# A new instruction order for a linear-attention and feed-forward kernel: w2 issued third by third behind w1, other chunks transposed by DMA

## The chip, the cores and the metric

The kernel runs on one core of a Trainium2 chip. The metric is the device time of one execution in microseconds (us). The inputs and the output are float32 in HBM; the matrix work on the core is done in bfloat16.

## What is computed

Two stages, one after the other, cut to what matters:

```
# stage 1: B=4, H=8 heads, S=768 steps, D=48; state is D x D per head
for t in range(S):
    y[:, :, t] = r_t @ (state + outer(u * k_t, v_t))
    state      = w * state + outer(k_t, v_t)
# stage 2: x = y as rows of C = 384
xn  = (x - mean) / sqrt(var + 1e-6) * g_ln
out = x + relu(xn @ w1) @ w2          # w1: 384 x 1536, w2: 1536 x 384
```

## The kernel before, in words

The 4 x 768 rows are cut into 24 chunks of 128 rows, six for each batch entry. Chunk i goes through a row of named steps, each a small function; the order of all steps is written out by hand in the string PLAN (lines 20 to 92), one entry "step,index,engine". Every engine runs its entries in this order and never overtakes (v is VectorE, DVE; s is ScalarE, ACT; g is GpSimd, POOL; a dash leaves the engine to the step: TensorE, PE, or the DMA queue of SyncE, SP). A loop at lines 651 to 653 only reads the string and calls the steps. An entry waits for whatever its data need; everything behind it on its engine waits too.

The steps of a chunk, in the order of its data:

- LK, LR, LV (lines 346 to 353) load k, r, v in 192-byte rows, 192 KB each, through SP's queue into rings of ten buffers.
- SK, SR (355 to 359) multiply k and r by powers of w into bf16 sck and scr. CV (361) casts v to vv.
- TR (364) transposes scr and sck on PE, eight matmuls against an identity; TC, TCr, TCk (371 to 378) copy the result from PSUM into trs. For chunks named in K_BY_DMA, TR does only scr and TKD (526) transposes sck by DMA; where the plan has TRD (530), scr goes by DMA too.
- Q (395) is an elementwise product for the u term in chunks 0 to 8. From chunk 9 on, KU and KR (389, 392) and a sum in CC replace it.
- AT (398) makes the 128 x 128 scores per head on PE, AM (426) masks them out of PSUM on DVE into A.
- S (429) makes the chunk's addition to the state in PSUM. ZU, ZD (460, 467) decay it into Z. For chunks in ZPE, PE adds the earlier Z itself by an identity matmul (line 441), so that ZU alone does it.
- VB (470), Y (476) and X (495) give x, with its row sum.
- SQ, XN, RS (501 to 520) do the normalization; g_ln is folded into w1.
- LT (534) and XT (539) transpose xn on PE and copy it out; LTD (522) does it by DMA instead.
- UP (543) multiplies by w1, RL (560) applies relu, DN (572) multiplies by w2, OT (634) adds, STO (641) stores. The last chunk is stored in two halves (DA, DB, OA, OB, SA, SB).

GROUPS joins chunks for UP: a group of one chunk does an UP of 12 matmuls of 128 columns, three of them covering the hidden width; a group of two does six UP of six matmuls of 256 columns. An entry UP,16g+m is part m of group g; DN,4i+d is third d of chunk i. UP's PSUM tile hp has two buffers, each freed by an RL.

The weights come in thirds. LW1 (line 329) loads a third of w1 (768 KB, 2 KB rows) on SP's queue. SW (332) scales one third of a third, index 3n+kc, into bf16 w1_sb on the engine that the plan names. IW2 (343) loads a third of w2 with a cast to bf16; it is issued from POOL and goes through POOL's own DMA queue. UP for a third of the hidden width needs that third's three SW; DN,4i+d needs third d of w2.

WU and DU are matmuls on zeros that nobody reads, put where PE would be idle.

Of the kernel before, what the change touches and what calls it, by code (L numbers as in the profile page):

```python
# [20 lines left out]
MW,0,v WF,0,- TL,0,s MI,0,g WU,13,- MP,0,v LN,0,s MM,0,g LK,0,- WBM,0,- RI,0,s LR,0,-
FR,0,s LV,1,- DU,4,- CL,0,- FK,0,s SR,0,v LK,2,- SK,0,v WL,0,s DU,3,- TR,0,- LR,1,-
UR,0,g TCk,0,v LK,1,- SK,2,g DU,2,- CU,0,- TCr,0,s SR,1,v LV,0,- Q,0,v AT,0,- UGC,0,s
LR,2,- SK,1,v AMb,0,v DU,3,- TR,1,- CV,0,s LK,3,- UW,0,s AMa,0,v S,0,- SR,2,v LV,2,-
Y,0,- TC,1,v CC,0,s LW1,1,- DU,9,- AT,1,- ZU,0,v VB,0,g Q,1,v CV,1,g X,0,v DU,9,-
TR,2,- CV,2,g S,1,- XN,0,g TC,2,s AM,1,v LR,3,- IW2,0,g SW,3,s LW1,0,- CC,1,v IW2,1,g
Q,2,v DU,13,- Y,1,- SW,4,s ZU,1,v LT,0,- VB,1,g SK,3,v SQ,0,s DU,1,- S,2,- SR,3,g
DU,1,- AT,2,- X,1,v XT,0,s AM,2,v XN,1,s SW,5,g DU,6,- TR,3,- CC,2,s SQ,1,s IW2,2,g
TC,3,v DU,1,- UP,1,- SW,2,v SW,1,s SW,0,g AT,3,- ZU,2,v LT,1,- RL,1,s Y,2,- AM,3,v
LV,3,- VB,2,g UP,0,- XT,1,s RS,0,g LK,4,- RL,0,s X,2,v DU,1,- UP,16,- CV,3,s XN,2,g  # L30
DN,0,- LW1,2,- RS,1,g SQ,2,s Q,3,v Y,3,- LT,2,- RL,16,s S,3,- SK,4,v XT,2,s CC,3,v
UP,33,- ZU,3,v VB,3,g UP,32,- RL,33,s SW,7,g X,3,v UP,17,- SW,8,g RL,32,v XN,3,s LR,4,-
RL,17,s SW,6,g LT,3,- LK,5,- DN,1,- XT,3,v RS,2,g UP,34,- SR,4,v LR,5,- SQ,3,s UP,2,-
RL,34,s RS,3,g SK,5,v LV,4,- TR,4,- RL,2,s UP,50,- SR,5,g TC,4,s UP,49,- RL,50,s AT,4,-
RL,49,s TR,5,- Q,4,v CV,4,s UP,18,- AM,4,v LV,5,- TC,5,s ZD,3,g S,4,- UP,48,- CC,4,v
LV,6,- VB,4,g ZU,4,v DN,2,- RL,48,s Q,5,v LR,6,- ZD,4,g Y,4,- OT,0,v AT,5,- RL,18,s
X,4,v S,5,- LK,6,- DN,4,- CV,5,g CC,5,v AM,5,v XN,4,s DN,5,- LK,7,- SQ,4,s VB,5,g
LT,4,- DN,6,- SR,6,v XT,4,s SK,6,g LR,7,- Y,5,- CV,6,v UP,65,- LUB,0,- UP,66,- SK,7,g
OT,1,v LR,8,- X,5,v TR,6,- RL,65,s DN,8,- SR,7,v LK,8,- TC,6,s RS,4,g RL,66,v UP,64,-
LV,7,- XN,5,v AT,6,- Q,6,v RL,64,s TR,7,- SR,8,v LR,9,- SK,8,g S,6,- TC,7,s DN,9,-  # L40
AM,6,v LK,9,- DN,10,- SQ,5,s CC,6,v Q,7,v LT,5,- LV,8,- VB,6,g CV,7,s Y,6,- ZU,6,v
AT,7,- XT,5,s OT,2,v S,7,- RS,5,g STO,1,- TR,8,- X,6,v LWB,0,- DN,12,- CC,7,v SK,9,v
XN,6,s VB,7,g LK,11,- DN,13,- ZU,7,v AM,7,v UP,82,- ZD,7,g LK,10,- TC,8,s DN,14,- UWR,0,v
SQ,6,s LK,12,- Y,7,- Q,8,v LT,6,- RL,82,s KU,9,v SR,9,g AT,8,- X,7,v STO,0,- XT,6,s
UP,80,- AM,8,v XN,7,s LV,10,- CV,8,g TR,9,- SQ,7,s SK,10,g S,8,- LK,13,- OT,3,v UP,81,-
TC,9,s KR,9,v RS,6,g Y,8,- SK,11,v LV,9,- DN,16,- RL,81,s KU,10,g LT,7,- LR,16,- DN,17,-
CC,8,v RL,80,v XT,7,s CV,9,s CC,9,v DN,18,- CV,10,g STO,2,- KU,11,v VB,8,g UP,101,- LR,10,-
ZU,8,v OT,4,v AT,9,- VB,9,g RL,101,s STO,3,- UP,98,- X,8,v LK,15,- AM,9,v S,9,- ZD,8,g
XN,8,s UP,96,- RL,98,s LV,11,- DN,20,- SK,12,v RL,96,s ZU,9,v Y,9,- SQ,8,s LK,18,- LT,8,-
SR,10,v UP,97,- ZD,9,g XT,8,s X,9,v LV,12,- DN,21,- KR,10,v RL,97,s S,10,- XN,9,v CV,11,s  # L50
TR,10,- LR,11,- KU,12,v DN,22,- CC,10,v SK,13,g TC,10,s LR,13,- ZU,10,v UP,100,- ZD,10,g UP,99,-
SQ,9,s LR,12,- OT,5,v LT,9,- RL,100,s AT,10,- VB,10,g LR,20,- XT,9,s DN,24,- AM,10,v SR,13,g
RL,99,s UP,112,- LK,14,- UP,117,- SR,11,v CV,12,s LV,14,- Y,10,- SR,12,g RL,112,v S,12,- DN,25,-
X,10,v LV,13,- KR,11,g RL,117,v TR,11,- SQ,10,s UP,114,- STO,4,- TC,11,s CC,11,v LR,17,- DN,26,-
KR,12,v VB,11,g KU,13,v RL,114,s TR,12,- XN,10,s LR,15,- RS,7,g UP,115,- CC,12,v TC,12,s ZU,12,v
AT,11,- LV,15,- VB,12,g OT,6,v UP,113,- CV,13,s RL,115,v KR,13,g TR,13,- CV,14,s LV,19,- AM,11,v
DN,28,- SK,15,g TC,13,s STO,5,- DN,29,- LR,14,- RL,113,v SK,14,g Y,11,- CC,13,v LT,10,- DN,30,-
CV,15,s LK,16,- X,11,v KU,15,g XT,10,s UP,116,- XN,11,s OT,7,v STO,6,- SR,15,g AT,12,- KU,14,v
RL,116,s LV,16,- LT,11,- DN,32,- SQ,11,s SR,14,g AM,12,v S,13,- LR,18,- XT,11,s DN,33,- RS,8,g
UP,128,- KR,14,v LK,17,- VB,13,g UP,129,- ZU,13,v LV,17,- CC,14,v Y,12,- ZD,13,g DN,34,- RL,129,s  # L60
X,12,v CV,16,s LK,19,- S,14,- SR,16,v TR,14,- RL,128,s KR,15,g AT,13,- TC,14,s LV,18,- OT,8,v
UP,133,- AM,13,v SK,16,g DN,36,- LR,19,- RL,133,s TR,15,- SR,17,v XN,12,s VB,14,g STO,8,- DN,37,-
CC,15,v TC,15,s STO,7,- SR,18,v UP,132,- VB,15,g SQ,12,s LK,21,- Y,13,- UP,130,- RL,132,s ZU,14,v
KU,16,g CV,17,s LTD,12,- X,13,v AT,14,- RL,130,s DN,38,- XN,13,v ZD,14,g SQ,13,s AM,14,v UP,131,-
TKD,16,- TR,16,- RS,9,g RL,131,s S,15,- OT,9,v AT,15,- LTD,13,- KR,16,g Y,14,- ZU,15,v DN,40,-
AM,15,v TCr,16,s ZD,15,g S,16,- DN,41,- LK,20,- CV,18,s X,14,v SK,17,g AT,16,- STO,9,- ZU,16,v
UP,145,- XN,14,s LK,22,- CC,16,v UP,144,- SQ,14,s SK,18,v VB,16,g DN,42,- RL,145,s TRD,17,- KU,17,v
RL,144,s Y,15,- KU,18,g UP,149,- OT,10,v TKD,17,- KR,17,v DN,44,- CV,19,g RL,149,s X,15,v DN,45,-
SR,19,g CC,17,v SQ,15,s TRD,18,- AM,16,v UP,146,- XN,15,g UP,148,- RS,10,g LTD,14,- SK,19,v RL,146,s
DN,46,- UP,147,- SK,20,v LTD,15,- OT,11,v AT,17,- ZD,16,g Y,16,- DN,48,- RL,147,s TKD,18,- AM,17,v  # L70
RL,148,s S,18,- VB,17,g DN,49,- X,16,v UP,160,- SR,20,g TRD,19,- XN,16,s Y,17,- ZU,18,v SK,21,g
UP,164,- SQ,16,s TKD,19,- X,17,v AT,18,- RL,160,s KR,18,v KU,19,g DN,50,- XN,17,s LTD,16,- RL,164,s
UP,162,- OT,12,v KR,19,g UP,165,- CC,18,v RL,162,s STO,11,- AM,18,v DN,52,- VB,18,g SQ,17,s LTD,17,-
S,19,- DN,53,- RL,165,v Y,18,- KU,21,g UP,161,- KU,20,v LR,23,- UP,163,- RL,161,s CC,19,v KR,20,g
STO,10,- AT,19,- ZU,19,v LV,20,- UP,177,- RL,163,v VB,19,g CC,20,v DN,54,- TRD,20,- ZD,19,g RL,177,v
UP,178,- OT,13,v RS,11,g UP,179,- TKD,20,- RL,178,s AM,19,v DN,56,- UP,176,- CV,20,v LR,21,- X,18,v
DN,57,- RL,176,v SR,23,g SQ,18,s LV,21,- Y,19,- RL,179,v DN,58,- XN,18,g X,19,v LR,22,- UP,181,-
VB,20,g OT,14,v AT,20,- STO,12,- SK,22,v XN,19,g DN,60,- SQ,19,s AM,20,v STO,13,- S,20,- KU,22,g
LTD,18,- DN,61,- RL,181,s CV,21,v DN,62,- SR,22,g ZU,20,v LTD,19,- UP,180,- OT,15,v RS,12,g Y,20,-
RL,180,s DN,64,- TKD,21,- ZD,20,g X,20,v DN,65,- KR,22,v S,21,- DN,66,- LK,23,- SQ,20,s XN,20,v  # L80
SR,21,g UP,194,- OT,16,v UP,193,- CC,22,v RL,194,s STO,14,- SK,23,g DN,68,- STO,15,- UP,192,- TRD,22,-
RS,13,g RL,193,s DN,69,- KR,21,v CC,21,v UP,195,- TRD,21,- RL,192,s DN,70,- RL,195,s UP,196,- KU,23,g
LV,22,- OT,17,v AT,21,- VB,21,g DN,72,- STO,16,- RL,196,s AM,21,v KR,23,g UP,197,- LTD,20,- DN,73,-
VB,22,g RL,197,s ZU,21,v Y,21,- TKD,22,- CV,22,g DN,74,- X,21,v ZD,21,g S,22,- CC,23,v UP,210,-
XN,21,s LV,23,- OT,18,v SQ,21,s AT,22,- ZU,22,v DN,76,- TKD,23,- RL,210,s RS,14,g AM,22,v UP,209,-
VB,23,g DN,77,- LTD,21,- ZD,22,g Y,22,- RL,209,s UP,208,- X,22,v TRD,23,- CV,23,g UP,226,- RL,208,s
DN,78,- STO,17,- SQ,22,s RL,226,v UP,224,- OT,19,v AT,23,- RS,15,g DN,80,- AM,23,v XN,22,s DN,81,-
DN,82,- STO,18,- Y,23,- LTD,22,- RL,224,s OT,20,v UP,225,- X,23,v DN,84,- RL,225,s STO,19,- UP,240,-
XN,23,s DN,85,- DN,86,- SQ,23,s UP,242,- LTD,23,- RL,240,s OT,21,v UP,241,- RL,242,v RS,16,g STO,20,-
# [594 lines left out]
```

## Time and profile before

| what | value |
|---|---|
| median of 9 runs | 153.62 us (152.39 to 154.54) |
| profiled execution | 153.06 us |
| its span, first to last instruction | 151.2 us |
| mean granted TensorE clock | 0.997 |
| busy: PE, PEld, DVE, ACT, POOL | 141.9, 114.0, 118.3, 84.6, 102.8 us |
| DMA moved | 26.25 MB in 93578 packets |
| w1 third: issue to landing, median of 3 | 9.9 us |
| w2 third: issue to landing, median of 3 | 7.6 us |

The span lies within the profiled execution's time; the rest is start and end around it. Busy time on PE overlaps from one matmul to the next, so that a busy PE need not be a PE at its peak; PEld is the loading of matmul weights, beside the matmuls. SPq stands for SyncE's DMA queue. A wait in the profile is the idle time of an engine just before an instruction, with what ended it.

### The profile page before, as it was taken

What the parts mean: (1) busy time and instruction counts of PE and PEld (TensorE: products, weight loads), DVE (VectorE), ACT (ScalarE), POOL (GpSimd) and SP (SyncE); (2) the same over time, 40 slices, a digit from 0 to 9 for tenths busy, and PEclk for the clock granted to TensorE, in tenths of its full rate; (3) what the DMA queues carried; (4) which work ended last, traced back from release to release, by engine and by line L of the source; (5) the groups of instructions that cost most, each with busy time, mean ns of one, the idle gap of its engine ahead of it and who ended that gap; (6) DMA issues with size and microseconds to landing.
All of it is one profiled execution on the core that took longest, in us unless ns stands there. A gap on an engine that the chain in (4) does not pass through costs nothing.

```text
span 151.2 us, 4453 instructions
## 1 busy us (share of the span) xinstructions
PE 141.9 (94%) x1769; PEld 114.0 (75%) x1769; DVE 118.3 (78%) x228; ACT 84.6 (56%) x172; POOL 102.8 (68%) x143
## 2 busy tenths in 40 slices
...
GB/s 82 223 218 294 306 236 279 185 205 171 186 183 182 190 261 191 210 237 155 252 216 217 162 149 136 75 92 105 209 201 149 208 165 125 76 122 52 130 56 52
DMA packets 93578, 26.25 MB, mean 174 GB/s; under 512 B 88563, under 2 KB 92022, under 8 KB 93558
## 3 DMA queue, kind: packets, MB, share of 16 engines
...
q10 hardware_dynamic: 4, 0.00, 0.0%
...
## 4 chain that ended last, share of the span: by engine, by line
PE 62%; DVE 13%; SPq 10%; DMA 8%; issue 2%; POOL 2%; ACT 1%; DVEq 0%
PE o L580 25%; PE hp L552 25%; DMA w_f<-in_moe_w_ch_dram 8%; DVE A L413 4%; SPq L347 4%; PE at L403 3%; SPq L353 2%; PE y L489 2%; PE tr L369 2%; SPq L350 2%; DVE q L209 2%; DVE scr L209 2%; PE y L481 2%; POOL w_sb L341 2%; SPq L330 1%
## 5 line engine op out<-in xcount | busy, mean ns | idle before, releaser
L552 PE MATMUL hp<-xT,w_sb 128*128 128x128 bf16 (+1 forms) x612 | 56.9, 241 | 1.1 <-POOL w_sb L341 0.8
L580 PE MATMUL o<-w_sb,hT 128*128 128x384 bf16 x276 | 54.2, 326 | 0.2
L552 PEld LDWEIGHTS <-w_sb 128*128 128x128 bf16 x612 | 48.5, 113 | 5.5 <-POOL w_sb L341 1.1
L568 ACT ACTIVATE hT<-hp 128x512 bf16<-128x512 f32 x56 | 32.9, 594 | 34.6 <-PE hp L552 34.4
L580 PEld LDWEIGHTS <-hT 128*128 128x128 bf16 x276 | 24.7, 98 | 12.0 <-issue 0.2
L413 DVE TENSOR_TENSOR A<-at,mask 128x1024 bf16<-128x1024 f32 (+1 forms) x25 | 29.2, 1171 | 3.0 <-PE at L403 3.0
L471 POOL TENSOR_TENSOR Vb<-vf,cc 128x384 f32<-128x384 f32 x24 | 21.3, 891 | 12.2 <-DVE cc L206 5.9
L636 DVE SCALAR_TENSOR_TENSOR ot<-o,rs,x 128x384 f32<-128x384 f32 x23 | 14.1, 611 | 8.0 <-PE o L580 7.5
L503 ACT ACTIVATE sqj<-x,sm 128x384 bf16<-128x384 f32 x24 | 14.6, 610 | 5.1 <-DVE x L496 5.1
L204 ACT COPY trs<-tr 128x1024 bf16<-128x1024 bf16 (+1 forms) x15 | 14.3, 952 | 5.5 <-PE tr L369 4.3
L496 DVE SCALAR_TENSOR_TENSOR x<-y,Vb 128x384 f32<-128x384 f32 x24 | 13.2, 549 | 3.8 <-PE y L489 2.2
L209 POOL TENSOR_TENSOR Z<-ZS,WLZ 128x384 bf16<-128x384 f32 x14 | 14.5, 1036 | 2.2 <-PE y L489 1.2
L209 POOL TENSOR_TENSOR sck<-kf,Fk 128x384 bf16<-128x384 f32 x12 | 12.3, 1035 | 2.6 <-DMA kf<-in_k_dram 1.5
L209 POOL TENSOR_TENSOR scr<-rf,Fr 128x384 bf16<-128x384 f32 x12 | 12.8, 1072 | 2.0 <-DMA trs<-scr 1.1
L509 ACT ACTIVATE xn<-x,sm 128x384 bf16<-128x384 f32 x15 | 9.2, 615 | 8.7 <-DVE x L496 8.7
L570 DVE TENSOR_SCALAR hT<-hp 128x512 bf16<-128x512 f32 x16 | 10.9, 685 | 2.8 <-PE hp L552 2.5
L520 POOL TENSOR_TENSOR rs<-rs,expo 128x1 f32<-128x1 f32 (+1 forms) x17 | 10.8, 633 | 1.4
L209 DVE TENSOR_TENSOR scr<-rf,Fr 128x384 bf16<-128x384 f32 x12 | 8.7, 724 | 3.5 <-DMA rf<-in_r_dram 3.5
L403 PE MATMUL at<-trs 48*128 48x128 bf16 x192 | 10.0, 226 | 1.1 <-DVE trs L206 1.1
L517 POOL TENSOR_SCALAR rs<-sq 128x1 f32<-128x1 f32 (+1 forms) x17 | 4.0, 236 | 10.0 <-ACT sqj L503 8.9
L209 DVE TENSOR_TENSOR sck<-kf,Fk 128x384 bf16<-128x384 f32 x12 | 8.8, 740 | 1.6 <-DMA kf<-in_k_dram 1.6
L489 PE MATMUL y<-vv,A 128*128 128x48 bf16 x192 | 8.9, 185 | 0.2 <-DVE A L413 0.2
...
## 6 DMA issues: line engine op xcount, KB each, us to landing
...
```

Source lines behind the costliest of these rows:

```text
L204: nc.scalar.copy(out=out, in_=in_)
L209: engines[e].tensor_tensor(out=out, in0=in0, in1=in1, op=ALU.mult)
L403: nc.tensor.matmul(out=t[:, par, q, :], lhsT=trs(i)[p0 : p0 + D, 1, q, :], rhs=trs(i)[p0 : p0 + D, 0, q, :], start=True, stop=True,)
L413: nc.vector.tensor_tensor(out=AA(i)[:, a:b].rearrange("p e q t -> p (e q) t"), in0=psum["at", i][:, a:b].rearrange("p e q t -> p (e q) t") ...
L471: nc.gpsimd.tensor_tensor(out=Vb(i)[:].rearrange("p (h d) -> p h d", h=H), in0=vf(i)[:], in1=cc(i)[:].unsqueeze(2).to_broadcast([P, H, D]) ...
L489: nc.tensor.matmul(out=t[:, h * D : (h + 1) * D], lhsT=AA(i)[:, par, q, :], rhs=vv(i)[:, h, :], start=first, stop=True, skip_group_check=True,
L496: nc.vector.scalar_tensor_tensor(out=xx(i)[:], in0=psum["y", i][:, :C], scalar=1.0, in1=Vb(i)[:], op0=ALU.mult, op1=ALU.add, accum_out=sm[ ...
L503: nc.scalar.activation(out=sqj[:], in_=xx(i)[:], func=ACT.Square, bias=sm[i][:], scale=-float(C), accum_out=sq[g][:, j : j + 1])
L552: nc.tensor.matmul(out=t[:, a * gw : (a + 1) * gw], lhsT=w1_sb[n][kc][:, fb::FB], rhs=xT(g)[:, kc, :gw], start=(kc == 0), stop=(kc == CK - 1),
L568: nc.scalar.activation(out=o, in_=s, func=ACT.Relu)
L580: nc.tensor.matmul(out=psum["o", i][:, :C], lhsT=hT(g)[:, fk, j * P : (j + 1) * P], rhs=w2_sb[d][:, a, :], start=(fk == 0), stop=(fk == FK ...
L636: nc.vector.scalar_tensor_tensor(out=ot(i)[:], in0=psum["o", i][:, :C], scalar=rs[g][:, j : j + 1], in1=xx(i)[:], op0=ALU.mult, op1=ALU.add,)
```

## The change

No function changes, only three constants and the plan. Chunk 15's k goes by DMA too, while r of chunks 17, 18 and 19 is transposed on PE again (TRD stays for 20 to 23). Chunks 12 and 13 get LT instead of LTD. ZPE now has chunks 3 and 4. The last four chunks are a pair and two singles.

```
-GROUPS = [1, 1, 1, 1, 1, 1, 2, 2, 2, 2, 2, 2, 2, 1, 1, 1, 1]
-ZPE = [1, 2]
-K_BY_DMA = [16, 17, 18, 19, 20, 21, 22, 23]
+GROUPS = [1, 1, 1, 1, 1, 1, 2, 2, 2, 2, 2, 2, 2, 2, 1, 1]
+ZPE = [1, 2, 3, 4]
+K_BY_DMA = [15, 16, 17, 18, 19, 20, 21, 22, 23]
```

All 71 lines of PLAN are replaced by 72. Taken apart by engine, the head of the two plans reads as follows (a step with its index; warm-up matmuls DU with their count).

```
SP before:   WF LK0 LR0 LV1 LK2 LR1 LK1 LV0 LR2 LK3 LV2 LW1,1 LR3 LW1,0 LV3 LK4 LW1,2 LR4 LK5 LR5 ...
SP after:    WF LK0 LR0 LR1 LK1 LK2 LR2 LV0 LK3 LV1 LR3 LW1,0 LV2 LW1,2 LV3 LW1,1 LR4 LK4 LK5 LUB ...
POOL before: ... SK2 VB0 CV1 CV2 XN0 IW2,0 IW2,1 VB1 SR3 SW5 IW2,2 SW0 VB2 RS0 XN2 RS1 VB3 SW7 SW8 SW6 ...
POOL after:  ... SK2 SR2 SR3 VB0 SW0 IW2,0 VB1 IW2,1 SW8 IW2,2 VB2 SW3 SW5 SW4 RS0 VB3 RS1 RS2 SR4 ...
PE before:   ... LT0 DU1 S2 DU1 AT2 DU6 TR3 DU1 UP1 AT3 LT1 Y2 UP0 DU1 UP16 DN0 Y3 LT2 S3 UP33 UP32
             UP17 LT3 DN1 UP34 UP2 TR4 UP50 UP49 AT4 TR5 UP18 ...
PE after:    ... Y1 DU30 LT0 DU1 S2 UP0 AT3 DU2 Y2 LT1 UP2 S3 DU2 UP16 UP18 Y3 LT2 UP17 UP1 DN0 UP33
             UP32 LT3 DN1 UP34 DN2 UP48 UP50 DN4 DN5 DN6 TR4 UP49 DN8 AT4 S4 TR5 ...
```

In the whole plan the steps are spread over the engines differently (count before, then after):

| step | before | after |
|---|---|---|
| RL | s 56, v 16 | s 67, v 5 |
| SR | v 12, g 12 | v 5, g 19 |
| SK | v 12, g 12 | v 11, g 13 |
| KU | v 7, g 8 | v 13, g 2 |
| KR | v 8, g 7 | v 9, g 6 |
| CV | s 13, g 8, v 3 | s 22, g 1, v 1 |
| TC | s 13, v 2 | s 10, v 4 |
| TCr, TCk | s 2, v 1 | s 5, v 2 |
| XT | s 11, v 1 | s 9, v 5 |
| XN | s 15, g 5, v 4 | s 17, g 4, v 3 |
| ZD | g 14 | g 12 |
| SW | g 5, s 3, v 1 | g 5, s 2, v 2 |
| LT, LTD | 12, 12 | 14, 10 |
| TKD, TRD | 8, 7 | 9, 4 |
| DU matmuls | 53 | 81 |

In the tail PE's order before ends UP224 AT23 DN80 to DN82 Y23 UP225 DN84 UP240 ... UP256 UP257 UP258 and the two halves; after, Y23 stands ahead of DN76, and the last parts are UP226, UP240, UP241 and UP242.

More of the change, by code (lines that the diff above doesn't have):

```diff
@@ L20 @@
 PLAN = """
[L21 to L89, printed above, removed]
@@ L90 @@
-DN,88,- RL,241,s UP,256,- STO,21,- DN,89,- RL,256,v DN,90,- UP,257,- OT,22,v UP,258,- RL,257,v DA,0,-
-RL,258,s DA,1,- DA,2,- STO,22,- DB,0,- DB,1,- OA,23,v DB,2,- OB,23,v SA,23,- SB,23,-
+MW,0,v WF,0,- TL,0,s MI,0,g WU,13,- MP,0,v MM,0,g LN,0,s LK,0,- WBM,0,- RI,0,s LR,0,-
+CL,0,- FR,0,s LR,1,- FK,0,s SR,0,v LK,1,- WL,0,s SK,0,v SR,1,v LK,2,- UR,0,g DU,10,-
+TR,0,- SK,1,v LR,2,- CU,0,- TCk,0,s SK,2,g LV,0,- TCr,0,s UGC,0,s LK,3,- DU,4,- AT,0,-
+Q,0,v UW,0,s SR,2,g CV,0,s LV,1,- AMb,0,v DU,2,- TR,1,- AMa,0,v S,0,- LR,3,- TC,1,s
@@ new lines @@
+CC,0,v ZU,0,v LW1,0,- Q,1,v DU,11,- TR,2,- CV,1,s AT,1,- SK,3,v S,1,- SR,3,g AM,1,v
+DU,1,- Y,0,- TC,2,s VB,0,g Q,2,v DU,11,- TR,3,- LV,2,- AT,2,- X,0,v SW,2,s LW1,2,-
+AM,2,v DU,7,- Y,1,- XN,0,s SW,0,g CV,2,s IW2,0,g SW,1,v TC,3,v CC,1,s LV,3,- SQ,0,s
+VB,1,g ZU,1,v DU,30,- LT,0,- IW2,1,g XT,0,s LW1,1,- DU,1,- S,2,- X,1,v SW,6,s SW,8,g
+UP,0,- Q,3,v XN,1,s IW2,2,g AT,3,- SW,7,v SQ,1,s DU,2,- Y,2,- CC,2,v CV,3,s ZU,2,v
+LT,1,- VB,2,g UP,2,- RL,0,s SW,3,g S,3,- X,2,v XT,1,s RL,2,s SW,5,g AM,3,v DU,2,-
@@ new lines @@
+UP,16,- XN,2,s UP,18,- SW,4,g RL,16,v SQ,2,s Y,3,- RS,0,g CC,3,v RL,18,s LT,2,- UP,17,-
+ZU,3,v VB,3,g XT,2,s UP,1,- RL,17,v RS,1,g DN,0,- RL,1,s X,3,v RS,2,g UP,33,- XN,3,s
+UP,32,- SQ,3,s LR,4,- LT,3,- RL,33,s DN,1,- RL,32,s LK,4,- UP,34,- XT,3,s DN,2,- SR,4,g
+RL,34,v LK,5,- UP,48,- OT,0,v LUB,0,- UP,50,- SK,4,v LR,5,- SK,5,v DN,4,- RL,50,s RS,3,g
+DN,5,- LV,4,- RL,48,s DN,6,- LR,6,- TR,4,- OT,1,v UP,49,- LWB,0,- CV,4,s TC,4,v SR,5,g
+DN,8,- LK,6,- RL,49,s Q,4,v AT,4,- UWR,0,v S,4,- LV,5,- SR,6,g AM,4,v TR,5,- DN,9,-
@@ new lines @@
+LV,6,- TC,5,s SK,6,g CC,4,v DN,10,- ZU,4,v LR,7,- CV,5,s AT,5,- Q,5,v CV,6,s TR,6,-
+OT,2,v LK,7,- VB,4,g S,5,- Y,4,- AM,5,v CC,5,s DN,12,- VB,5,g LK,8,- TC,6,s DN,13,-
+X,4,v SR,7,g LV,8,- XN,4,s Y,5,- DN,14,- Q,6,v SQ,4,s SK,7,g LR,8,- X,5,v LT,4,-
+AT,6,- XT,4,v XN,5,s S,6,- RS,4,g STO,0,- AM,6,v TR,7,- CV,8,s LV,7,- UP,66,- SK,8,g
+TC,7,s OT,3,v UP,64,- LR,9,- SR,8,g RL,66,s AT,7,- CC,6,v SQ,5,s LT,5,- LK,9,- Q,7,v
+UP,65,- XT,5,v RL,64,s RS,5,g Y,6,- STO,1,- TR,8,- RL,65,s AM,7,v SR,9,g DN,16,- LR,17,-
@@ new lines @@
+TC,8,s UP,81,- ZU,6,v VB,6,g STO,2,- CV,7,s DN,17,- Q,8,v LR,10,- SK,9,g X,6,v S,7,-
+DN,18,- CC,7,v SQ,6,s LV,9,- ZU,7,v VB,7,g Y,7,- KU,9,v XN,6,s TR,9,- LV,10,- ZD,7,g
+RL,81,s S,8,- OT,4,v UP,80,- TC,9,s KR,9,v LK,10,- AT,8,- SR,10,g X,7,v CC,8,s UP,82,-
+RL,80,s AM,8,v LK,13,- SQ,7,s VB,8,g DN,20,- XN,7,s LK,19,- LT,6,- CV,10,v RS,6,g AT,9,-
+ZU,8,v CV,9,s DN,21,- XT,6,s AM,9,v LK,11,- ZD,8,g RL,82,s S,9,- LT,7,- Y,8,- XT,7,s
+LK,12,- CC,9,v DN,22,- SK,10,g X,8,v UP,99,- LR,11,- OT,5,v XN,8,s VB,9,g UP,101,- ZU,9,v
@@ new lines @@
+RL,99,s LV,12,- SK,11,v TR,10,- ZD,9,g SQ,8,s RL,101,v UP,96,- TC,10,s STO,3,- KU,11,v S,10,-
+UP,97,- LR,16,- KU,10,v RL,96,s KR,10,v SR,11,g LT,8,- AT,10,- ZU,10,v XT,8,s LV,15,- UP,98,-
+CC,10,v RL,97,s SK,13,g AM,10,v Y,9,- LR,12,- TR,11,- VB,10,g DN,24,- X,9,v LR,14,- TC,11,s
+UP,100,- RL,98,v ZD,10,g STO,5,- SK,12,v Y,10,- XN,9,s DN,25,- KR,11,g LR,15,- RL,100,s X,10,v
+LT,9,- SQ,9,s DN,26,- SR,12,v LV,11,- XT,9,s SR,14,g AT,11,- OT,6,v UP,117,- LR,13,- XN,10,s
+CC,11,v RS,7,g UP,113,- AM,11,v RL,117,s LV,13,- DN,28,- SQ,10,s VB,11,g KU,12,v LT,10,- CV,11,s
@@ new lines @@
+LK,14,- UP,115,- SR,13,g XT,10,v CV,12,s KR,12,v DN,29,- RL,113,s LK,15,- CV,13,s KU,13,v UP,112,-
+CC,12,v RL,115,s STO,4,- KR,13,v Y,11,- RL,112,s LR,18,- TR,12,- SK,14,v CV,15,s S,12,- X,11,v
+DN,30,- SR,15,g LV,14,- TC,12,v XN,11,s UP,116,- OT,7,v VB,12,g LK,16,- LT,11,- AT,12,- ZU,12,v
+UP,114,- SQ,11,s SK,15,g AM,12,v LV,16,- RL,116,s S,13,- DN,32,- RS,8,g XT,11,s LV,21,- ZU,13,v
+Y,12,- RL,114,s UP,130,- KU,14,v CV,14,s KR,14,v STO,6,- ZD,13,g DN,33,- CC,13,v LR,19,- TR,13,-
+CC,14,v VB,13,g UP,128,- KU,15,v LV,22,- RL,130,s SK,16,g S,14,- TC,13,v DN,34,- LK,18,- KR,15,v
@@ new lines @@
+UP,129,- VB,14,g OT,8,v TR,14,- LV,23,- RL,129,s KU,16,v AT,13,- SR,16,g X,12,v TC,14,s DN,36,-
+LK,17,- CC,15,v DN,37,- AM,13,v XN,12,s SR,17,g LV,17,- RL,128,s TR,15,- DN,38,- SQ,12,s KR,16,g
+ZU,14,v STO,7,- Y,13,- TCr,15,v CV,16,s LV,19,- UP,132,- OT,9,v ZD,14,g X,13,v S,15,- UP,131,-
+LR,20,- VB,15,g CC,16,v RL,132,s AT,14,- ZU,15,v SQ,13,s SK,17,g LV,18,- DN,40,- AM,14,v RL,131,s
+UP,133,- ZD,15,g STO,8,- XN,13,s LT,12,- KU,17,v TKD,15,- DN,41,- RL,133,s RS,9,g XT,12,v Y,14,-
+CV,17,s KR,17,v LT,13,- DN,42,- SR,18,g TKD,16,- XT,13,v X,14,v UP,145,- SK,18,g XN,14,v SQ,14,s
@@ new lines @@
+AT,15,- LK,20,- S,16,- RL,145,s UP,146,- AM,15,v TKD,17,- UP,147,- RL,146,s TR,16,- VB,16,g RL,147,s
+OT,10,v UP,144,- LTD,14,- TCr,16,s KU,18,v CV,18,g DN,44,- SK,19,v Y,15,- RL,144,s LR,21,- KR,18,v
+TR,17,- KU,19,g X,15,v DN,45,- CV,19,s CC,18,v XN,15,s STO,10,- UP,148,- SR,20,g CC,17,v STO,9,-
+DN,46,- RL,148,s VB,17,g TKD,18,- ZU,16,v UP,149,- OT,11,v SK,20,g TCr,17,s AT,16,- DN,48,- LTD,15,-
+SQ,15,s AM,16,v ZD,16,g TR,18,- RL,149,s DN,49,- TCr,18,s LV,20,- RS,10,g Y,16,- AT,17,- SR,21,g
```

21 lines of the change are left out of this document (added).

## The prediction

> **What bounds the kernel now.** I read the page first, then the busy times of each engine in six stretches, then the chain that ended last, then the POOL and PE timelines around 16 to 31 us, then the two DMA queues in short windows.
>
> The six stretches are cut at the points where the chain changes its character. Columns: stretch, length, busy us (and instructions) of PE, PEld, DVE, ACT, POOL, then granted clock, DMA share, GB/s.
>
> ```profile
> 0.00:15.88 15.88, 14.84 (x168) 12.40 (x169) 9.31 (x28) 6.06 (x14) 6.57 (x18) 1.00 0.93 213
> 15.88:19.59 3.71, 2.50 (x49) 1.90 (x47) 3.71 (x4) 2.29 (x5) 3.65 (x6) 1.00 1.12 269
> 19.59:30.39 10.80, 8.20 (x133) 6.69 (x131) 8.29 (x19) 7.67 (x18) 7.06 (x11) 1.00 1.03 236
> 30.39:54.84 24.45, 23.56 (x373) 19.52 (x374) 21.70 (x40) 16.65 (x31) 17.77 (x25) 1.00 0.90 189
> 54.84:147.68 92.84, 92.80 (x1055) 73.53 (x1054) 74.83 (x140) 51.95 (x106) 67.71 (x86) 1.00 0.73 156
> ```
>
> From 54.84 us to the last matmul at 147.68 PE never waits (92.80 of 92.84). There only the amount of PE work counts. From 30.39 to 54.84 it is nearly dense. What is left to win lies before 30.39, and the chain says what holds it (start, length, what):
>
> ```profile
> 13.16 2.62 SPq L347
> 15.83 12.02 DMA w_f<-in_moe_w_ch_dram
> 27.94 2.40 POOL w_sb L341 x3
> 30.39 1.54 PE hp L552 x24
> ```
>
> The last third of w1 is issued at 15.83, takes 12.0 us to land, is scaled by three POOL instructions, and only then does PE start its dense run. Why 12 us for 768 KB? The queues in two windows, 18 to 22 us and 22 to 26 us (q0 is POOL's queue, which carries w2; q1 is SP's; then packets, MB, share of the 16 DMA engines):
>
> ```profile
> q0 software_dynamic: 249, 0.68, 85.8%
> q1 hardware_dynamic: 796, 0.17, 23.9%
> ```
> ```profile
> q1 hardware_dynamic: 774, 0.76, 56.2%
> q0 software_dynamic: 149, 0.40, 50.6%
> ```
>
> While w2 flows, the SP queue with its 192-byte packets of v and k keeps a quarter of the engines. With 2 KB packets of w1 the two alternate one for one: between 23 and 25 us the one-microsecond windows show 48 and 53 q1 packets beside 46 and 50 of q0. Without w2 the 12 to 13 us window passed 160 packets of w1. So w2, issued from 14.89 us, is what delays the last third.
>
> **Part 1, the head.** Ahead of the first third both orders put ten loads of k, r and v, so it lands as now: the first scaling starts at 15.88. Then the old SP order is r3, w1, v3, k4, w1; the new one v2, w1, v3, w1. One 192 KB load (k4, which landed only 12.6 us after issue) leaves the front. I take the issue at k4's place, 13.16, finished by 15.8 at the latest, since a w1 third has 384 packets to k4's 1024.
>
> POOL's order becomes SK2, SR2, SR3, VB0, SW0, IW2 0, VB1, IW2 1, SW8, IW2 2, VB2, SW3, SW5, SW4. SR3 waits for r3, now tenth in the queue; the tenth load landed near 13.7 (POOL's cast of v2 began 13.75). Adding 1.0 for SR3 and 0.8 for VB0 gives 15.55; SW0 waits for w1 until 15.9 and ends at 16.6; IW2 0 follows. Issue to first q0 packet was 14.89 to about 17.4 us, 2.5 us, so w2 flows from 19.1 instead of 17.4. SW0 is the new wait; behind it on POOL stand IW2 0 and VB1, and X1 on DVE waits for VB1. I carried that through: VB1 at 17.6 (after CC1 on ACT), ZU1 at 18.4, S2 and UP0 on PE near 19.3, against 19.59 for the first UP now.
>
> v3's packets were 340 in the 16 to 17 us window and 648 in the next, so with w2 later v3 is through by 18.0. Then w1's last third has 1.1 us alone: 1.1 x 160 = 176 of its 384 packets. The other 208 alternate with w2 at about 50 per us, 4.2 us: landing 23.3, against 27.85.
>
> Here a rule speaks against the change. The Trainium skill (DMA: Bandwidth & Descriptors, section "Issuing engines are not separate DMA queues") says that transfers started by any engine share the same 16 DMA engines and interleave, and that starting them on several engines saves only issue time. Taken alone, moving w2 on its queue wins no bandwidth, which is right: shares add to one, and w2 will end near 27 us in either order (27.0 now). But it leaves open who gets how much. An equal split of the bytes (half of some 0.28 MB per us) would bring the remaining 0.43 MB in 3.0 us, landing 22.1. The row gives a q1 packet only one turn per q0 packet of about 2.7 KB, hence 4.2 us and 23.3. I take the row; the rule would make the time 1.2 us less.
>
> After the landing, SW3, SW5 and SW4 run on POOL as three do now (27.94 to 30.39, 2.45 us): UP17 starts at 25.75. VB2, ahead of them, is done near 21.1 (CC2 at 20.0 plus 0.8). Before UP17, PE has UP0, 2, 16 and 18, LT2 and Y3. That path runs X2 21.6, A3 22.75, Y3 and LT2, ending near 24.0, so it doesn't bind, and the thirty warm-up matmuls (1.6 us) lie before S2, which waits for ZU1 anyway. PE idles some 1.7 us here.
>
> Now count work. At 30.39 the old order had done six UP, two DN and LT0 to LT3; at its UP17 the new one has done four UP, no DN and LT0 to LT2. Missing: 2 x 0.655 + 2 x 0.65 + 0.17 = 2.78 us (from the chain: UP 0.66, DN 0.65, LT 0.17). Gain of the head: 30.39 - 25.75 - 2.78 = 1.86 us.
>
> **Part 2, PE work added.** Chunk 15's k goes to DMA: 4 transposes less, -0.22. r of 17, 18 and 19 comes back to PE: +3 x 0.22. LT of 12 and 13 replaces two DMA transposes: +2 x 0.17. Z by the identity matmul in chunks 3 and 4: 0.16 each, of which chunk 3's falls into the wait of the head; +0.16. Together +0.94 us, all in the stretch where PE never waits, so all on the path. Groups: eight pairs and eight singles instead of seven and ten; an UP costs 0.65 us in both (12 x 128 columns or 6 x 256), three per chunk: nothing.
>
> **Part 3, work moved between engines.** By counts and row means: DVE loses 11 RL (0.69) and 7 SR (0.72), gains 6 KU (0.71), 4 XT and some TC, about -7 us of 118. ACT gains 11 RL (0.59) and 9 CV (0.51) and loses three TC, about +9 on 85. POOL gains 7 SR (1.07) and a SK, loses 7 CV, 6 KU, 2 ZD, about -5 of 103. SP issues 23 transposes instead of 27, at 1.2 to 1.5 us each, so SP gets freer. All stay under PE's 95%: cost nothing while PE work covers them. If ACT is late for one RL, PE stands after two UP, since hp has two buffers; a miss costs about 0.6 us. The transposes that stay (landing median 2.4 us for xT) have cover: LTD15 has about 6.2 us of PE work between Y15 and UP160 against 4.7 us of X, XN, issue and landing; LTD23 has 7.2 us.
>
> **Part 4, the stretch after the head.** From 30.39 to 54.84 PE had 12 UP, 10 DN, 6 TR, 5 AT, 5 S, 5 Y and 3 LT, 22.9 us of issue (AT with the 0.11 us that follows each), so 1.6 us were lost to DVE, which the chain names there. The new order puts seven UP, six DN and LT3 ahead of TR4 and has SK4, SK5 done. Stepping chunks 4 to 7 with the row durations I find almost no stall, at best -1.6 us; at worst SQ, XN and TC queue on ACT and the same amount comes on top. I take -0.4.
>
> **Sum** against the profiled execution: span 151.2 - 1.86 + 0.94 - 0.4 = 149.9. It took 153.06 with what lies around the span (1.9), so 151.7; the median is 0.56 above that execution: 152.3.
>
> **Rivals.** (a) *The last third comes too late.* If v3 still has 500 packets when w2 begins (SP's issue stuck, as k5's was for 5.8 us), they go at 200 per us (816 small packets in 4 us), 2.5 us, and w1 then meets w2 for nearly all of its way: landing at 26 to 27. The head breaks even with Part 2 and 4 at a landing of 24.6; every us after that is a us lost, since PE does nothing meanwhile. Landing 26.5 gives 155.5. For it: the SP queue's stuck issues, and that the margin is only 1.3 us. Against it: v3 was nearly through by 18 us even with w2 beside it.
> (b) *Moved, not removed.* The wait for w1 shrinks, but DVE and ACT then bound the pace of chunks 4 to 8, and part of the head's gain is given back before 55 us: of the 1.6 us lost there, not 1.2 stay but 2.4 come, 152.3 + 1.2 = 153.5. For it: DVE sat at 5.00 of 5 us from 35 to 55 us. Against: it has 7 us less to do.
> (c) *The floor of the head.* w2 starts later than I think and the third lands by 21.5; then LT2 at 24.0 binds, 1.75 us earlier than 25.75: 150.6 (149.4 if all 1.6 us of the next stretch go too). For it: the equal split above; against it: the one-for-one packets.
>
> **How the numbers follow.** Forecast 152.3, its own range 151.4 to 152.9, chance 0.37; (c) 0.12; (b) 0.21; (a) 0.30. A measurement of this kernel can tell about 0.5%, 0.77 us, from no change. The forecast case and (c) lie almost wholly below 152.85: faster 0.47; (b) and a sliver of others: same 0.21; (a) and the upper end of (b): slower 0.32. The range goes down to (c) and up to (a): 150.6 to 155.5.
>
> **What would show it.** Right: last w1 landing near 23.3 (24.6 breaks even); first UP near 19.3; POOL's three scalings end near 25.75 and PE dense from there; q0's first packets near 19; from 55 us PE without waits; PE's work about 0.9 us longer. Wrong: q1 at a quarter of the DMA engines with v3 still in it after 19 us; PE waits for ACT's hT or trs after 55 us; a transpose by DMA named as what ended an idle time of PE. If PE has gaps in 55 to 147 us, Part 3's cover was missing, and the forecast is wrong even if the head does as said.

## The result, and the profile after

The new order takes 152.54 us (median of 16 runs, 151.42 to 153.36), the kernel before 154.06 (51 runs): ratio 0.9918, 95% interval 0.9894 to 0.9941. On two other chips the same kernel came out at 0.9957 (0.9912 to 1.0001) and 0.9924 (0.9878 to 0.9971); the first of these intervals just includes no change. Ratios, and the medians given with the experiments below, leave out executions more than 1.5% above the fastest of the same kernel, so that 0.9918 is not the quotient of the two medians above. The profiled execution took 152.16 us with a span of 149.9, which is the predicted span to the digit. That is luck: the spans of the 16 runs go from 149.2 to 151.1, and several terms of the sum were wrong and cancelled.

The stretches again, cut at the new kernel's own turning points (columns as before: stretch, length, busy us of PE, PEld, DVE, ACT, POOL, granted clock, DMA share, GB/s):

```profile
15.88:19.59 3.71, 3.71 (x74) 3.32 (x72) 3.60 (x9) 2.71 (x8) 3.23 (x5) 1.00 1.09 358
19.59:24.58 4.99, 4.99 (x105) 4.71 (x102) 4.47 (x12) 4.99 (x13) 4.43 (x8) 1.00 1.13 237
24.58:30.39 5.81, 5.81 (x85) 5.08 (x83) 2.18 (x6) 3.77 (x9) 4.17 (x9) 1.00 0.88 182
30.39:54.84 24.45, 24.45 (x369) 19.23 (x367) 22.11 (x42) 18.07 (x36) 18.92 (x24) 1.00 1.00 209
54.84:86.14 31.30, 31.10 (x362) 25.13 (x359) 31.09 (x63) 22.73 (x47) 27.06 (x32) 1.00 1.01 213
86.14:88.03 1.89, 0.82 (x8) 0.55 (x7) 0.80 (x3) 1.19 (x3) 0.66 (x1) 1.00 0.57 79
88.03:109.15 21.12, 21.12 (x238) 16.91 (x239) 16.24 (x30) 13.97 (x29) 19.28 (x24) 1.00 0.73 154
109.15:110.52 1.37, 0.34 (x7) 0.19 (x4) 1.37 (x3) 0.00 (x0) 0.91 (x1) 1.00 0.51 99
110.52:146.95 36.43, 36.40 (x388) 28.78 (x388) 18.51 (x37) 17.40 (x35) 11.02 (x17) 1.00 0.37 95
```

PE is dense from 15.88 us on (part of that is warm-up matmuls), loses nothing up to 54.84, and then stands twice, at 87 and at 109 us. The kernel before had it the other way round: gaps early, none late.

The head in POOL's timeline (start, length, engine, line, what, and the idle time ahead with what ended it):

```profile
16.04 0.69 POOL L342 TENSOR_SCALAR w_sb<-w_f,g_neg 128x512 bf16<-128x512 f32 x1 [0.95 <-DMA w_f<-in_moe_w_ch_dram]
16.68 0.79 POOL L345 DMA_DIRECT2D w_sb<-in_moe_w_ch_dram  x1
17.73 1.03 POOL L472 TENSOR_TENSOR Vb<-vf,cc 128x384 f32<-128x384 f32 x1 [0.27 <-ACT cc L205]
...
20.97 0.82 POOL L472 TENSOR_TENSOR Vb<-vf,cc 128x384 f32<-128x384 f32 x1 [0.39 <-DVE cc L207]
21.79 2.02 POOL L342 TENSOR_SCALAR w_sb<-w_f,g_neg 128x512 bf16<-128x512 f32 x3
```

The three scalings of the last third follow VB2 without a wait: the third had landed (8.2 us after its issue, at 21.55, against 27.85 before). The issue, in SP's timeline:

```profile
13.35 2.66 SPq L331 DMA_DIRECT2D w_f<-in_moe_w_ch_dram  x1
```

UP17 starts at 24.58, when Y3 and LT2 are done. The DMA queues say why it came so early. From 19 to 20 us, then from 20 to 21 and 21 to 22, each as packets, MB, share of the 16 DMA engines:

```profile
q1 hardware_dynamic: 374, 0.35, 104.5%
```
```profile
q1 hardware_dynamic: 679, 0.20, 81.0%
q0 software_dynamic: 28, 0.09, 43.3%
```
```profile
q0 software_dynamic: 59, 0.18, 91.9%
q1 hardware_dynamic: 101, 0.02, 11.1%
```

Before, q0 had 84.2% and q1 29.9% in the 19 to 20 us window. Now SP's queue has the DMA engines to itself there, with w1 and the first small packets behind it, and w2 begins when w1 is nearly through. From 23 to 24 us w2 has the small packets beside it:

```profile
q0 software_dynamic: 70, 0.20, 99.1%
q1 hardware_dynamic: 68, 0.01, 11.4%
```

The two late gaps, in PE's timeline:

```profile
88.03 0.40 PE L404 MATMUL at<-trs 48*128 48x128 bf16 x8 [1.07 <-DMA trs<-sck]
```
```profile
110.52 0.37 PE L490 MATMUL y<-vv,A 128*128 128x48 bf16 x8 [1.03 <-DVE A L414]
```

The first is AT15, which waits for the DMA transpose of chunk 15's k. That one is new. In SP's timeline:

```profile
82.50 0.65 SPq L644 DMA_DIRECT2D out_dram<-ot  x1
83.25 4.11 SPq L529 DMA_TRANSPOSE trs<-sck  x2
```

It is the first DMA transpose of the kernel, is issued behind the store of chunk 8 at 83.25, and lands 4.7 us later, at 87.98. The second gap is Y19, which waits for AM19. In DVE's timeline:

```profile
108.18 1.15 DVE L210 TENSOR_TENSOR ku<-sck,uw_b 128x384 bf16<-128x384 bf16 x1 [1.68 <-POOL sck L210]
109.25 1.21 DVE L414 TENSOR_TENSOR A<-at,mask 128x1024 bf16<-128x1024 f32 x1
```

AM19 could start when AT19 is done, at 106.6 (in PE's timeline AT19 starts at 106.20 and lasts 0.40); it stands behind KU21, which waits 1.68 us for POOL's SK21.

### The profile page after: what moved, and what is told of

Read it like the earlier page. It is cut to its first block, busy times and chain, and to the rows that moved or that the text cites. A ratio compares the mean times of both kernels' runs of the same rounds, so it can differ in the third digit from the quotient of the medians.

```text
span 149.9 us, 4473 instructions
## 1 busy us (share of the span) xinstructions
PE 143.6 (96%) x1777; PEld 116.4 (78%) x1777; DVE 109.8 (73%) x220; ACT 92.6 (62%) x192; POOL 96.2 (64%) x132
## 4 chain that ended last, share of the span: by engine, by line
PE 67%; POOL 11%; DVE 10%; issue 5%; DMA 4%; ACT 1%; POOLq 0%; DVEq 0%
PE hp L553 22%; PE o L581 21%; PE tr L370 5%; PE o L263 4%; PE at L404 4%; DMA trs<-sck 3%; DVE A L414 3%; POOL Vb L472 3%; PE y L490 2%; POOL scr L210 2%; DVE ku L210 2%; PE s L449 2%; DVE x L497 1%; POOL sck L210 1%; PE y L482 1%
## 5 line engine op out<-in xcount | busy, mean ns | idle before, releaser
L569 ACT ACTIVATE hT<-hp 128x512 bf16<-128x512 f32 x67 | 39.4, 595 | 29.4 <-PE hp L553 28.5
L210 POOL TENSOR_TENSOR scr<-rf,Fr 128x384 bf16<-128x384 f32 x19 | 20.1, 1059 | 8.5 <-DMA rf<-in_r_dram 7.1
L210 POOL TENSOR_TENSOR sck<-kf,Fk 128x384 bf16<-128x384 f32 x13 | 13.6, 1046 | 5.9 <-ACT trs L205 2.8
L205 ACT COPY trs<-tr 128x1024 bf16<-128x1024 bf16 (+1 forms) x15 | 12.9, 869 | 6.5 <-PE tr L370 6.2
L210 POOL TENSOR_TENSOR Z<-ZS,WLZ 128x384 bf16<-128x384 f32 x12 | 12.5, 1044 | 2.4 <-DVE ZS L466 2.2
L205 ACT CAST vv<-vf 128x384 bf16<-128x384 f32 x22 | 11.1, 508 | 3.4 <-PE y L490 2.9
L510 ACT ACTIVATE xn<-x,sm 128x384 bf16<-128x384 f32 x17 | 10.4, 612 | 2.2 <-DVE x L497 2.2
L263 PE MATMUL o<-warm 128*128 128x128 bf16 x94 | 9.4, 258 | 1.0 <-DVE warm L228 1.0
L518 POOL TENSOR_SCALAR rs<-sq 128x1 f32<-128x1 f32 (+1 forms) x16 | 3.1, 191 | 10.7 <-ACT sqj L504 9.7
L404 PEld LDWEIGHTS <-trs 48*128 48x128 bf16 x192 | 5.5, 96 | 5.2 <-issue 1.9
```

The costliest lines, as they stand in the source:

```text
L205: nc.scalar.copy(out=out, in_=in_)
L210: engines[e].tensor_tensor(out=out, in0=in0, in1=in1, op=ALU.mult)
L263: nc.tensor.matmul(out=warm_ps[0][:, :P], lhsT=warm[:], rhs=warm[:], start=True, stop=True)
L404: nc.tensor.matmul(out=t[:, par, q, :], lhsT=trs(i)[p0 : p0 + D, 1, q, :], rhs=trs(i)[p0 : p0 + D, 0, q, :], start=True, stop=True,)
L569: nc.scalar.activation(out=o, in_=s, func=ACT.Relu)
```

## The experiments

My theory after this: (1) what stands ahead of the last third of w1 in the two DMA queues makes the head faster; (2) chunk 15's transpose costs both late gaps, the second through SK18, which must wait for its buffer. The rivals: the gain comes from steps moved between engines; POOL or ACT is the bound late, whatever chunk 15 does. Times are medians beside the kernel before on the same chip.

### e3: k of chunk 4 back ahead of the last third

```
-... LV3 LW1,1 LR4 LK4 ...
+... LV3 LK4 LW1,1 LR4 ...
```

> The new order with one load moved back: k of chunk 4 stands ahead of the last third of w1 again, as before. Theory (what stands ahead of the third on SP's queue when w2 begins decides): k's 1024 small packets start near 18 us, meet w2 at 19 and are let through one for one, so the third begins only near 22 and lands near 26; UP17 starts near 28 instead of 24.6, and the time is 2.5 to 3.5 us above the new order, ratio to before 1.01. Rival (192 KB are 0.9 us of transfer, wherever they stand): landing at most 1 us later, which the floor of PE's other work half hides; time within 0.7 us of the new order.

Measured 158.17 us, ratio 1.024 (1.016 to 1.032): 4.4 us above the new order on that chip (e0, 153.72), from moving one 192 KB load. POOL's timeline, then PE's:

```profile
26.58 2.02 POOL L342 TENSOR_SCALAR w_sb<-w_f,g_neg 128x512 bf16<-128x512 f32 x3 [4.28 <-DMA w_f<-in_moe_w_ch_dram]
```
```profile
27.32 0.25 PE L553 MATMUL hp<-xT,w_sb 128*128 128x128 bf16 x1 [2.08 <-POOL w_sb L342]
28.66 1.57 PE L553 MATMUL hp<-xT,w_sb 128*128 128x128 bf16 x13 [1.09 <-POOL w_sb L342]
```

POOL waits 4.28 us for the landing at 26.5, and PE's dense run starts at 28.66. The last of k's packets crawl beside w2 (from 20 to 21 us SP's queue passed 16 packets, w2 62). Much of the third then passes while w2 hardly flows (22 to 23 us: 184 packets, 0.38 MB, beside one of w2), its end beside w2 again. The landing and the late UP17 are as the theory had them (26 and 28), and the rival falls. This is also the slower case of the prediction, made to happen.

The time is longer than the theory's 2.5 to 3.5 us, and the clock is part of it, which I had not reckoned with. While PE stood, the granted clock fell to half for 3.4 us (a stretch of the trace, columns as before):

```profile
28.49:31.90 3.41, 3.24 (x26) 2.88 (x27) 1.16 (x3) 0.56 (x2) 2.90 (x8) 0.50 1.00 211
```

The 23 matmuls that start at 28.66 take 2.64 us; the same 23 take 1.48 us in e2's trace, at full clock. Half of 3.4 us, up to 1.7 us, is my estimate of what the clock cost in this execution, whose mean clock is 0.989. All four executions of e3 are at 0.989 or 0.978, so the 4.4 us are not the late landing alone.

### e2: the first two thirds of w2 issued early again

```
-... VB0 SW0 IW2,0 VB1 IW2,1 SW8 ...
+... VB0 IW2,0 IW2,1 SW0 VB1 SW8 ...
```

> The new order with the first two thirds of w2 issued ahead of the first scaling on POOL, near 15 us, as the kernel before does. Theory (w2's packets take the turns of w1's): q0 flows from 17.5 us, v3's small packets get stuck behind it, the last third of w1 lands near 25 to 26 instead of 21.3 us, and PE's dense run starts near 27.5 instead of 24.6: about 3 us above the new order, ratio to before 1.01. Rival (all transfers share the same engines, so the order of issue hardly matters): landing within 1.5 us, time within 1 us of the new order, ratio 0.990 to 0.998.

Measured ratio 0.9991 (0.9948 to 1.0033), from only two executions (153.79 and 153.84 us), about 0.7% or 1.1 us above the new order as first measured. The two others took 157.70 and 158.58 us at a mean granted clock of 0.978; they have no trace, so what happened there is not known. In the profiled execution, one of the first two, the last third lands at 24.0 and POOL waits 2.39 us for it; the dense run of PE starts at 26.16. The direction is the theory's, the size a third of it: issued at 16.04, w2's first packets came only at 20.2 us, so most of the third had passed by then. The rival's landing (within 1.5 us) is wrong too. How long after its issue w2 begins to flow is thus not a constant, see the end.

### e4: only the DMA order of the head, put into the kernel before

```
-SP:   ... LV3 LK4 LW1,2 ...
+SP:   ... LV3 LW1,2 LK4 ...
-POOL: ... XN0 IW2,0 IW2,1 VB1 SR3 SW5 IW2,2 SW0 VB2 ...
+POOL: ... XN0 VB1 SR3 SW5 IW2,0 SW0 IW2,1 VB2 IW2,2 ...
```

> The kernel before, with nothing changed but the head's DMA order: k of chunk 4 behind the last third of w1, and w2's thirds issued behind the scaling on POOL. Every other step stays on its engine. Theory (the order of the weight loads is what made the head faster): the last third of w1 lands near 21.5 instead of 27.9 us; 1.5 to 2.5 us below before, less than the new order's head because DN0 now waits for w2, which lands near 24; ratio 0.985 to 0.990. Rival (the gain comes from steps moved between engines and from PE's order, not from the loads): the third lands earlier but the time is that of before, ratio 0.997 to 1.003.

Measured ratio 1.0029 (0.9984 to 1.0074): nothing won. The third landed at 21.6 us, as the theory said, and nobody could use it. PE's timeline, then POOL's:

```profile
25.31 1.14 PE L580 MATMUL o<-w_sb,hT 128*128 128x384 bf16 x4 [2.12 <-DMA w_sb<-in_moe_w_ch_dram]
```
```profile
28.12 0.83 POOL L471 TENSOR_TENSOR Vb<-vf,cc 128x384 f32<-128x384 f32 x1 [2.80 <-DVE cc L206]
29.05 2.02 POOL L341 TENSOR_SCALAR w_sb<-w_f,g_neg 128x512 bf16<-128x512 f32 x3
```

In the old PE order DN0 stands ahead of UP33; it now waits 2.12 us for w2, and with PE in order everything behind it waits, S3 among it. Then CC3 and VB3 are late, and the scaling stands behind VB3: it ends at 31.07 instead of 30.33. Here too the clock fell to half once PE had stood:

```profile
25.66:29.07 3.41, 3.27 (x37) 2.80 (x36) 0.72 (x3) 0.48 (x1) 0.85 (x2) 0.50 1.13 218
```

That lengthens this trace, but not the verdict: the four of the six executions at 0.997 or more took 153.5 to 155.7 us, median 153.96, and the kernel before 153.95 on that chip. So the loads alone are not the head. With e3, which shows that they are needed, this leaves them together with the rest of the new head: PE's order (six UP ahead of the first DN, three before), POOL's (the three scalings directly behind VB2) and the steps moved between engines. The trace points at the first two; no run separates them from the third. My theory (1) was too narrow, and the rival's number came out.

### e1: chunk 15's k transposed on PE again

```
-K_BY_DMA = [15, 16, ...]        +K_BY_DMA = [16, ...]
-TCr,15,v ... TKD,15,-           +TC,15,v
```

> The new order with chunk 15's k transposed on PE again and no DMA transpose for it. Theory (the late transpose of chunk 15 costs both later stalls, the one at AT15 and, through SK18's wait for the buffer, the one at Y19): 2.4 us of stalls go, 0.22 us of PE work come back, so about 2.2 us below the new order, ratio to before 0.978 and a span of 147.7 us with PE never idle for 1 us after 55 us. Rival (POOL and ACT carry too much in that stretch whatever chunk 15 does): the gap at AT15 goes, the gap before Y19 stays, at most 1 us is won, ratio 0.985 or above.

Measured 152.24 us, ratio 0.9889 (0.9858 to 0.9921). The gap at AT15 is gone from its trace, the one before Y19 is there unchanged (1.04 us of wait). So the second gap does not come from chunk 15: that half of theory (2) falls, and the rival's numbers came out. The gain against the new order, 0.3%, lies inside the intervals.

### e5: the transpose of chunk 15 issued earlier

```
-STO7 LV19 LR20 LV18 STO8 TKD15 ...
+STO7 TKD15 LV19 LR20 LV18 STO8 ...
```

> The new order with only the DMA transpose of chunk 15's k moved on SP's queue, from behind three loads and the store of chunk 8 to just behind the store of chunk 7. Theory (its place in the queue makes it late, not that it is a DMA transpose): issued near 80 instead of 83.2 us, landed by 85, AT15 waits no more, SK18 neither; about 2.2 us below the new order, ratio 0.978. Rival (a DMA transpose among loads is slow wherever it stands, 4.7 us and more, and holds up the loads behind it): AT15 still waits, or a load of chunk 18 to 20 comes late instead; gain under 0.7 us, ratio 0.987 or above.

Measured ratio 0.9923 (0.9886 to 0.9961), which is the rival's number. SP's timeline:

```profile
81.66 1.29 SPq L529 DMA_TRANSPOSE trs<-sck  x1
```

AT15 ran at 89.48 with no wait. The DMA transposes around there landed at most 4.1 us after their issue, so this one had over 3 us to spare: in this trace its place in the queue decides. The time does not show it: this execution had a gap ahead of 73.62 us instead, where LT12 waits 1.19 us for XN on ACT, ahead of the edit, and the gap before Y19. Inconclusive on the time; on the cause it is one trace.

### e6, e7, e10: AM19 ahead of KU21, alone and with e1

```
-... SK22 KU21 AM19 KU22 ...     (DVE)
+... SK22 AM19 KU21 KU22 ...
```

> The new order with one step moved: KU21 on DVE stands behind AM19 instead of ahead of it. Theory (the gap before Y19 is a matter of order on DVE alone: AM19 stands behind KU21, which waits for POOL's SK21): AM19 follows AT19 at once, the gap of 1.2 us goes and KU21 has slack; 1.0 to 1.2 us below the new order, ratio to it 0.993. Rival (POOL is the bound there, whatever the order on DVE): the gap turns up one chunk later, where KR21 or VB waits on POOL, and the time is that of the new order within 0.3 us.

> The new order with both repairs: chunk 15's k transposed on PE, and KU21 behind AM19. Theory (two separate causes, each worth its gap): both gaps gone, 0.22 us more PE work, 2.0 us below the new order: ratio to before 0.979 and a span near 148. Rival (the time is given back elsewhere, as ACT and POOL run with little slack from 50 to 110 us): only 0.3 to 1 us below the new order, ratio 0.986 to 0.990.

> The version with both repairs (chunk 15's k on PE, KU21 behind AM19) a second time, for a narrower interval, and beside the new order on the same chip. Theory: 1.5 to 2.2 us below the new order, ratio to before 0.982. Rival: less than 0.8 us below it.

e6 alone: ratio 0.9866 (0.9822 to 0.9909), beside the unchanged new order at 0.9957 on that chip: 152.59 against 153.72 us, 1.1 us less, as its theory said. With e1's edit (e7): 0.9853 (0.9795 to 0.9911), 152.16 us, 1.6 us less, between the rival's 1 and the theory's 2.0. In a second set of runs (e10) 0.9805 (0.9734 to 0.9876), beside 0.9924 there: 151.88 against 153.59 us, 1.7 us less. That lies in the range of the theory of two separate causes. The gap before Y19 is gone from the traces of e6, e7 and e10. In e10's DVE timeline:

```profile
107.58 1.23 DVE L413 TENSOR_TENSOR A<-at,mask 128x1024 bf16<-128x1024 f32 x1
109.11 1.41 DVE L209 TENSOR_TENSOR ku<-sck,uw_b 128x384 bf16<-128x384 bf16 x2 [0.31 <-POOL sck L209]
```

KU21 still waits for POOL, now with nobody behind it who is urgent. The stretches of e10:

```profile
30.39:54.84 24.45, 23.32 (x344) 18.18 (x343) 20.04 (x40) 16.22 (x33) 17.17 (x22) 1.00 0.95 198
54.84:84.00 29.16, 28.85 (x350) 23.65 (x350) 28.76 (x56) 21.41 (x46) 25.11 (x29) 1.00 0.99 210
84.00:112.00 28.00, 28.00 (x320) 22.12 (x318) 24.16 (x50) 19.57 (x42) 25.06 (x32) 1.00 0.78 155
112.00:146.00 34.00, 33.97 (x361) 27.00 (x361) 16.67 (x33) 15.93 (x33) 11.02 (x17) 1.00 0.36 102
```

From 84 us on PE loses nothing. This version beats both kernels; the 1.1 us between 30 and 55 us lie mostly in one gap near 50 us, where PE waits 0.9 us for X on DVE. It is in four of the traces (e0, e5, e6, e10) and not in the others, whatever the edit.

### e8: more work for PE

```
-            for q in range(HP):
+            for q in [q for q in range(HP) for _ in range(2 if 6 <= i <= 14 else 1)]:
                 nc.tensor.transpose(...)
```

> The new order with every PE transpose of chunks 6 to 14 done twice into the same place: 72 matmuls of 56 ns more, 4.0 us of PE work between 38 and 80 us. Theory (PE is the bound there, so added PE work is on the path at its full price): 4.0 us longer, less up to 1.2 us for the gap at AT15, which then hides under it; 2.8 to 4.0 us above the new order. Rival (PE only looks busy, the pace is DVE's and the loads'): less than half of it shows, at most 1.5 us.

Measured 155.45 us, ratio 1.0034 (0.9992 to 1.0075), beside 153.59 for the new order: 1.9 us for 4.0 us of work, under the theory's 2.8 and over the rival's 1.5. The traces of the two on this chip tell where it went: spans 153.1 and 151.1; the new order had gaps of 1.25 us at AT15 and 0.95 us at 68 us, both gone in e8. 4.0 - 2.2 = 1.8, near the 2.0 of the spans. PE work is paid, but part of it fills gaps, and every trace of the unchanged new order has two or three of them.

### e9: eight RL back on DVE

```
-RL33, RL32, RL50, RL48, RL49, RL66, RL64, RL65 on ACT
+the same on DVE
```

> The new order with eight RL between 26 and 48 us back on DVE instead of ACT: 8 x 0.69 = 5.5 us more DVE work and 4.7 us less on ACT in this stretch. Theory (from 30 to 55 us the new order loses 0.4 instead of 2.0 us because DVE has less to do there): DVE becomes the bound again before 55 us, 1 to 2 us above the new order. Rival (what removed the losses is that the head hands PE a stock of UP and DN work ahead of TR4): within 0.6 us of the new order.

Measured 153.94 us, ratio 0.9961 (0.9911 to 1.001), beside 153.59 for the new order: 0.35 us more, which is the rival's number and under the theory's 1 to 2. The stretch in the new order on that chip (e11), then in e9:

```profile
30.40:54.84 24.44, 24.44 (x371) 19.23 (x369) 21.99 (x42) 17.76 (x36) 18.59 (x24) 1.00 0.98 205
30.40:54.84 24.44, 23.99 (x347) 18.18 (x345) 23.41 (x46) 14.04 (x29) 17.99 (x24) 1.00 1.00 211
```

PE loses 0.45 us there with DVE at 23.41, so DVE's load counts for something, but e0 and e10 lose 1.1 us there without this edit. My theory falls in its size: DVE's lighter load is not the main reason why the early losses went. The rival fits, that PE has UP and DN in stock ahead of TR4; no run removed that stock by itself, so it stays argued.

### e0, e11: the new order again

> The new order unchanged, for comparison on the same chip. Both theories: ratio to before 0.992 as first measured; its profile shows the two late gaps of PE again, about 1.2 us each, at AT15 and at Y19. If they depend on chance in the transfers, the one at AT15 varies and the one at Y19 stays.

> The new order unchanged, beside the other three. Both theories: ratio to before 0.992 to 0.996, and the gap before Y19 of about 1.2 us in its profile.

Measured 0.9957 and 0.9924, as told above. The gap before Y19 was 1.00 and 1.20 us there, and between 1.0 and 1.2 in all nine traces with the old place of KU21 (gaps are counted here from the end of the last matmul's issue, so they are a little longer than the waits in the views); the one at AT15 was 0.54 and 1.25. The first is fixed in the order. The second varies with unchanged order, down to nothing in e8, where the transpose landed within 3.2 us of its issue and PE came later.

## Why the prediction was right, step by step

- **Part 1, the head.** Right in kind, and the gain too small. Forecast: UP17 at 25.75, gain 1.86; measured 24.58, 3.03 us. The mis-sized term is the 208 packets of w1 that were to alternate with w2 for 4.2 us. I let w2 flow 2.5 us after its issue, from 19.1; its packets were first seen after 20.25, 3.6 us after its issue, when the third was nearly through. The landing was 21.55 instead of 23.3, and my own floor (LT2 near 24.0) took over: this is case (c), to which I had given a chance of 0.12. POOL's scalings took 2.02 us, not 2.45. The issue of the third (13.35, done by 16.0) and the first UP (19.71 for 19.3) were right.
- **The rule weighed there** (the Trainium skill, DMA: Bandwidth & Descriptors, "Issuing engines are not separate DMA queues"). The equal split gave a landing of 22.1, nearer to 21.55 than my 23.3, but for no reason of its own: the queues did not share the bytes, w2 was not there yet. The one-turn-each picture is borne out where both queues keep flowing, as from 23 to 24 us (70 packets beside 68, shown above). It is no constant: from 21 to 22 us SP's queue passed 101 packets beside 59 of w2, and in the prediction's own window of 18 to 22 us 796 beside 249 (case (a) counts 816 there; the view has 796).
- **Part 2, PE work.** Right. Counting each matmul with the time from its start to the next one's in dense stretches (0.056, 0.109 and 0.163 us for 128, 256 and 384 columns), the new order has 3.67 us more PE work from its UP17 on than the kernel before from 30.39 on, 0.89 us beyond the head's 2.78; forecast 0.94. e8 shows that such work is paid except where it fills a gap.
- **Part 3, moved work.** "Cost nothing while PE work covers them" failed in two places: the transpose of chunk 15's k came too late, and the order on DVE put AM19 behind a step that waits for POOL. I weighed engine totals (POOL 5 us less) and looked at two transposes by DMA, LTD15 and LTD23, but not at TKD15, the one that the change adds, nor at any masking step. With the gap at AT15 (1.23) and at Y19 (1.20) this cost 2.4 us; forecast was none. "PE without waits from 55 us" was a sign of being right that did not come, and a DMA transpose that ends a wait of PE was a sign of being wrong that did: by the prediction's own words this part of the mechanism was wrong.
- **Part 4, 30 to 55 us.** By the same count the lost time went from 1.9 to 0.5 us, a gain of 1.3 where I took 0.4. The stepping of chunks 4 to 7 had shown it; I did not trust it.
- **The sum.** Head -3.03, PE work +0.89, 30 to 55 us -1.34, small gaps from 55 to 84 us +0.53, the two late gaps +2.41, the rest up to the last matmul -0.18, from the last matmul to the end -0.57: together -1.29, and the span moved by -1.3. Forecast: -1.86 + 0.94 - 0.40 = -1.3. The number was right by cancellation, which is luck: the early gain was 2.1 us larger than forecast, and 2.9 us of late gaps were not seen; the shorter end, which no term covered and which I did not look into, makes up the rest.
- **Rivals.** (a) is real, as e3 shows, with 4.4 us, part of it the clock; its margin was wider than I said, since w2 came later. (c) came in its landing (21.5) but not in its time (150.6), because of the late gaps. (b) did happen in kind, the gain partly given back, but after 85 us and by order, not by the pace of chunks 4 to 8.
